# An adaLN attention and GEGLU block on one core: gate and up projections in seven products over two row groups, gates folded into the weights, and an order that knows which DVE and POOL instructions exclude each other

## The chip, the core and the metric

The kernel runs on one core of one Trainium2 chip. The metric is device time in microseconds (us), the median of three runs; there is one launch and no work on the host. The engines are PE (matrix products into PSUM), DVE and ACT (vector and scalar work, both read PSUM and SBUF), POOL (vector work on SBUF alone) and SP, which issues every DMA of this kernel.

## What is computed

```python
mod = (silu(c) @ w_mod).reshape(1, 6, 1, 512)          # sa, ca, ga, sb, cb, gb
h = layernorm(x) * (1 + ca) + sa                       # x: 2048 rows of 512
q = h @ wq                                             # 32 heads of 128
k, v = the last 512 rows of each head's cache
o = softmax(q @ k.T * 128 ** -0.5) @ v                 # every row sees all 512 keys
x = x + ga * (o @ wo)
h = layernorm(x) * (1 + cb) + sb
x = x + gb * ((gelu(h @ w_gate) * (h @ w_up)) @ w_down)   # 512 -> 1376 -> 512
```

## The kernel before

**Products in pairs.** Every large operand is held as two fp16 tiles, a high part and the rounding remainder (low part). A product is three fp16 matmuls into one PSUM bank: high x high, high x low, low x high. Nearly every matmul streams 512 columns. Making a pair is one ACT instruction (the high part) and one DVE or POOL instruction (value minus high part).

**Stages.** The 2048 rows are 4 row groups of 512. Attention goes over 16 pairs of heads, and for each over 2 heads x 4 row groups, 128 iterations in all, which overlap: scores (psS, two banks a tile, two tiles), maximum on DVE, exponentials on ACT, high part on ACT, low part on POOL, DMA transposes of the probabilities (pT), their product with v (psO), its pair (oT), and the product with Wo (psW), which DVE scales and adds to the 16 resident accumulators acc. From the fourth pair of heads on, the q projection of two heads and two row groups already uses seven half-size products in place of eight (PRODUCTS, with sums T1 to T4 of the activations and S1 to S4 of the weights).

Then comes the feed-forward part. For each row group acc is multiplied by ga and x is loaded again and added (x1_mul, x1_load, x1_add); the second layernorm gives a transposed pair (ln2_chunk, ln2_high, ln2_low); and for each of 11 blocks of 128 hidden columns (the last has 96) a *unit* follows: 24 gate and up matmuls into one psS tile, GELU on ACT, the product with up on DVE, the pair of the result (ff_act), and one unit later 12 matmuls with w_down into four banks that collect all 11 blocks (down). After the last block DVE multiplies by gb, POOL adds acc and the row group is stored. 4 row groups x 11 blocks are 44 units. All weight pairs are made in the first row group's units (ff_quick) and kept.

**Order.** The code doesn't issue instructions directly. A recorder (Weaver) notes each one with its operands (note), and a list scheduler (issue) then runs a small model of the engines with a cost for each instruction (cost) and emits on every engine what is ready and due first; each engine then takes its instructions strictly in that order. The recorder's line is that of every instruction in the profile (L245), so groups there are told apart by tile names. In those names numbers are left out: T and B are the named activation tiles, raw is a loaded weight block, wd a w_down pair, gl the GELU's output, hid or B its pair, y the output rows, and wm, mx, st small helpers.

## Time and profile before

| | us |
|---|---|
| median of 3 runs | 1748.34 (1746.94 to 1749.17) |
| the profiled execution, its own time | 1748.06 |
| its span, first to last instruction | 1746.3 |
| PE busy in the span | 1698.6 (97%) |
| DVE, ACT, POOL busy | 1213.4, 1081.5, 1069.3 (69, 62, 61%) |

The profile is one execution. A view by windows gives, for a stretch of the span, the busy time of each engine and the number of its instructions; a view by groups collects instructions of one kind and shape with their mean time; the timeline lists them in order, with the idle time before one and what ended it in square brackets. Attention fills the span from about 60 to about 1390 us, the feed-forward part the rest. A matmul's shown time includes its drain, during which the next one already runs, so rates are read from distances between starts.

### The profile page before, as it was taken

To read this page: it belongs to the slowest core of one execution; us is meant where nothing else is said; L and a number is where in the kernel's file an instruction comes from. 1 tells how busy PE (TensorE), PEld (TensorE's weight loads), DVE (VectorE), ACT (ScalarE), POOL (GpSimd) and SP (SyncE) were. 2 spreads that over 40 slices of the span, in tenths; PEclk is the share of its full clock that TensorE was granted. 3 is DMA by queue.
4 is the path that set the end of the run, shared out by engine and by line. 5 is a ranking of instruction groups with operands and counts; after the bars stand their busy time and mean duration, and the time that the engine had idled before them with its cause. 6 is when DMAs were issued, how large, how long until landed. Compare 5 with 4: busy or idle time off the path is not lost.

```text
span 1746.3 us, 23696 instructions
## 1 busy us (share of the span) xinstructions
PE 1698.6 (97%) x7927; PEld 785.7 (45%) x7927; DVE 1213.4 (69%) x2292; ACT 1081.5 (62%) x2145; POOL 1069.3 (61%) x845
## 2 busy tenths in 40 slices
...
GB/s 187 118 132 142 171 147 131 149 188 191 188 185 139 141 125 146 117 146 123 139 140 137 140 129 142 138 135 133 139 127 151 174 99 0 25 1 24 1 25 25
DMA packets 658955, 213.56 MB, mean 122 GB/s; under 512 B 580304, under 2 KB 640720, under 8 KB 658832
## 3 DMA queue, kind: packets, MB, share of 16 engines
...
q8 instruction: 63, 1.03, 0.2%
...
## 4 chain that ended last, share of the span: by engine, by line
PE 84%; DVE 6%; POOL 3%; DMA 3%; ACT 2%; issue 1%; SPq 0%; DVEq 0%; POOLq 0%; ACTq 0%
PE psS L245 30%; PE psW L245 19%; PE psO L245 19%; PE psQ L245 16%; DMA pT<-pp 3%; DVE st L245 2%; DVE acc L245 2%; POOL pp L245 1%; ACT p L245 1%; SPq L245 0%; ACT pp L245 0%; DVE mx L245 0%; DVE B L245 0%; POOL tf L245 0%; POOL A L245 0%
## 5 line engine op out<-in xcount | busy, mean ns | idle before, releaser
L245 POOL TENSOR_TENSOR pp<-p,pp 128x1024 f16<-128x1024 f32 x256 | 545.9, 2133 | 266.7 <-ACT pp L245 200.4
L245 ACT ACTIVATE p<-psS,st,es 128x512 f32<-128x512 f32 x512 | 393.1, 773 | 231.1 <-DVE st L245 224.6
L245 DVE SCALAR_TENSOR_TENSOR acc<-psW,st,acc 128x512 f32<-128x512 f32 x496 | 367.7, 743 | 120.5 <-PE psW L245 119.4
L245 PE MATMUL psW<-wo,oT 128*128 128x512 f16 x1536 | 416.4, 379 | 8.8 <-DVE oT L245 4.0
L245 PE MATMUL psS<-kT,q 128*128 128x512 f16 x1536 | 389.6, 381 | 1.1 <-DMA kT<-k 1.1
L245 PE MATMUL psO<-pT,v 128*128 128x512 f16 x1536 | 370.4, 379 | 8.1 <-DMA pT<-pp 7.7
L245 DVE TENSOR_REDUCE st<-psS 128x2 f32<-128x1024 f32 x256 | 312.7, 1222 | 79.9 <-PE psS L245 78.7
L245 ACT ACTIVATE pp<-p 128x1024 f16<-128x1024 f32 x256 | 270.7, 1058 | 3.6 <-DMA pT<-pp 0.9
L245 PEld LDWEIGHTS <-oT 128*128 128x128 f16 x1536 | 149.9, 98 | 190.9 <-issue 7.1
L245 PEld LDWEIGHTS <-v 128*128 128x128 f16 x1536 | 149.0, 98 | 192.8 <-issue 10.3
L245 PEld LDWEIGHTS <-q 128*128 128x128 f16 x1536 | 148.3, 98 | 173.3 <-issue 3.2
L245 ACT ACTIVATE gl<-psS,ffs 128x512 f32<-128x512 f32 (+1 forms) x44 | 30.2, 687 | 228.0 <-PE psS L245 228.0
L245 DVE SCALAR_TENSOR_TENSOR gl<-psS,ffs,gl 128x512 f32<-128x512 f32 (+1 forms) x44 | 32.9, 748 | 179.2 <-ACT gl L245 179.2
L245 ACT ACTIVATE oT<-psO 128x512 f16<-128x512 f32 x128 | 76.1, 594 | 90.1 <-PE psO L245 89.9
L245 PE MATMUL psQ<-B,A 128*128 128x512 f16 x528 | 130.2, 380 | 1.5 <-DVE q L245 1.5
L245 PEld LDWEIGHTS <-A 128*128 128x128 f16 x756 | 74.4, 99 | 97.1 <-issue 8.1
L245 PE MATMUL psQ<-T,S 128*128 128x512 f16 x468 | 114.6, 379 | 0.0
L245 PEld LDWEIGHTS <-B 128*128 128x128 f16 (+1 forms) x744 | 72.9, 98 | 86.0 <-issue 0.3
L245 DVE SCALAR_TENSOR_TENSOR oT<-psO,oT 128x512 f16<-128x512 f32 x128 | 87.8, 686 | 22.8 <-ACT oT L245 22.6
L245 PEld LDWEIGHTS <-T 128*128 128x128 f16 (+1 forms) x672 | 68.2, 101 | 77.2 <-issue 0.3
L245 ACT ACTIVATION_READ_ACCUMULATOR p<-psS,st,es 128x1 f32 x512 | 101.1, 197 | 0.0
L245 POOL TENSOR_TENSOR q<-h,q 128x512 f16<-128x512 f32 x78 | 90.2, 1157 | 13.8 <-ACT q L245 13.2
(194 smaller groups left out, 2062.2 us busy)
## 6 DMA issues: line engine op xcount, KB each, us to landing
...
pT<-pp SPq DMA_TRANSPOSE x512, 3.3
...
```

What stands on the lines that cost most here:

```text
L245: real(*a, **k)
```

## The change

**Seven products.** The gate and up projections of one block of hidden columns and *two* row groups become one *split unit*: with gate and up as the two rows and the two halves of the 512 inputs as the two columns of a 2 x 2 block matrix, and two row groups as the columns of the other factor, seven products of 6 matmuls each (42) stand for 48. Blocks 0 and 1 of the first two row groups stay as they were (PLAIN), so there are 4 plain units and 20 split units. The products come in four stages, (0, 6), (1), (2, 4), (3, 5), and collect in the two banks X and Y of a psS tile. After each of the first three stages ACT copies X to SBUF (h32) and DVE adds Y to such a copy (r, in stages one, three and four); GELU, product and pair follow. The activations need sums of half blocks (f_full, f_sum: ft and hf) and pairs of them (T1 to T4). The weights need four sums (aw_sum on POOL: S1f to S4f) and six pairs (aw_high on ACT, aw_low on POOL) for each of 16 split units; the 4 others use the pairs of the unit just ahead of them.

**w_down products.** Two blocks of hidden columns are collected in a bank (6 matmuls), and DVE adds the bank at once to acc, scaled by one number (down_add). acc is stored directly.

**Gates.** gb is multiplied into w_down on POOL (wd_gate) and, for the maxima that set the scale, once more during attention (fm_gate). ga is multiplied into Wo on POOL for the last 4 pairs of heads (h_gate), and into what acc has collected by then (acc_gate). x is loaded and added to acc during attention (x_load, x_add). The passes over acc between attention and the layernorm, y, and the passes over the output rows are gone.

**Order.** The scheduler's model takes new costs for SP (470 ns a load, 1290 ns a transpose, in place of 62) and for fp32 matmuls, a later landing of DMAs, a dependency between two engines that read one PSUM tile, and a lock: POOL instructions and DVE instructions with two SBUF operands (or tensor_scalar) don't overlap in it, and DVE takes another instruction first where it can.

In the program the 512-column matmuls go from 7574 to 7454, the 128-column transposes stay at 201.

```diff
-            return (110.0 if n > 8 else 60.0) * (1 if what == "transpose" or n <= 8 else n / 128) if wide else max(n, 60) / 2.4 + 2.4
+            if a[1].dtype != F32:
+                return max(n, 60) / 2.4 + 2.4
+            return 110.0 if what == "transpose" else 224.0 * max(1.0, n / 128)
...
+            alone = held[:1] == [None]
+            if alone:
                 lo, hi = -1, 1 << 30
             for e in held:
-                if e and (write or e[3]) and e[0] < hi and lo < e[1]:
+                if e and (write or e[3] or alone and self.ops[e[2]][0] != engine) and e[0] < hi and lo < e[1]:
...
+        d = (470.0 if what == "dma_start" else 1290.0) if engine == "SP" else self.cost(engine, what, a, k, n, [x.name for x in read])
+        if engine == "SP":
+            short = what == "dma_start" and any(len(x.ap) > 2 and list(x.ap)[-1][1] <= P for x in a[:2])
+            n = 1450.0 if what != "dma_start" else n * 4 * P / (195.0 if short else 390.0)
+        flat = [x for x in read if self.extent(x)[0] > 1]
+        lock = engine == "POOL" or (engine == "DVE" and not any(x.name.startswith("ps") for x in flat) and n > 2 and
+                                    (what == "tensor_scalar" or (len(flat) == 2 and what != "tensor_reduce")))
+        self.ops.append((engine, d, deps, real, a, k, n, lock))
...
-                lag = c if e == self.ops[n][0] == "PE" else c + self.LAG + (self.DRAIN if e == "PE" else 2600.0 if e == "SP" else 0.0)
+                lag = c if e == self.ops[n][0] == "PE" else c + self.LAG + (self.DRAIN if e == "PE" else 3300.0 if e == "SP" else 0.0)
...
-            n = heapq.heappop(can[e])[1]
+            aside = []
+            if e == "DVE" and shared > t + 100.0:
+                while can[e] and self.ops[can[e][0][1]][7]:
+                    aside.append(heapq.heappop(can[e]))
+                if not can[e] and wait[e] and wait[e][0][0] < shared:
+                    free[e] = wait[e][0][0]
+            pick = None if aside and free[e] > t else heapq.heappop(can[e]) if can[e] else aside.pop(0)
+            for x in aside:
+                heapq.heappush(can[e], x)
+            if pick is None:
+                continue
+            n = pick[1]
             order.append(n)
-            _, d, _, _, a, k, size = self.ops[n]
+            d, size, lock = self.ops[n][1], self.ops[n][6], self.ops[n][7]
+            if lock:
+                t = max(t, shared)
+                shared = t + d - self.NEXT[e]
             free[e] = t + d - self.NEXT[e]
...
-                whole = self.ops[n][3].__name__ == "dma_start"
-                bus = max(bus, t + 1350.0) + (size * 4 * 128 / 190.0 if whole else 1300.0)
-                end = max(bus, t + 2000.0) + 300.0
+                bus = max(bus, t + (1800.0 if d < 1000.0 else 1300.0)) + size
+                end = bus + 650.0
...
+    def h_gate(h):
+        nc.gpsimd.tensor_tensor(RAW["wo", h], RAW["wo", h], ga, op=OP.mult)
...
+                if kind == "wo" and g >= GATED:
+                    at(b + st[1], h_gate, h)
...
+    def fm_gate(n):
+        _, _, r, _ = pieces_[n]
+        m = r.stop - r.start
+        nc.gpsimd.tensor_tensor(FM[n][:m], FM[n][:m], gb[:m], op=OP.mult)
...
     for n in range(len(pieces_)):
-        at(s + 2 + 4 * n, fm_load, n)
-        at(s + 8 + 4 * n, fm_max, n)
-    s += 8 + 4 * len(pieces_)
+        at(s + 2 + 3 * n, fm_load, n)
+        if n >= 24:
+            at(s + 5 + 3 * n, fm_gate, n)
+        at(s + 8 + 3 * n, fm_max, n)
+    s += 8 + 3 * len(pieces_)
+
+
+    def acc_gate(t, eng):
+        eng.tensor_tensor(acc[t], acc[t], ga, op=OP.mult)
+
+    def x_load(t):
+        XR[t] = raw_tile("raw2", 2)
+        nc.sync.dma_start(XR[t], x[t * P:(t + 1) * P, :])
+
+    def x_add(t, eng):
+        eng.tensor_tensor(acc[t], acc[t], XR.pop(t), op=OP.add)
+
+    XR = {}
+    for t in range(SQ // P):
+        qg, j = divmod(t, 4)
+        at(2 * (PER * (GATED - 1) + 2 * qg + 5 + j) + 0.5, acc_gate, t, (nc.vector, nc.gpsimd)[j % 2])
+        at(s + 2 + 2 * t, x_load, t)
+        at(s + 8 + 2 * t, x_add, t, (nc.gpsimd, nc.vector)[t % 2])
...
+    def f_full(p, c, nm, eng):
+        t = FT[c, nm] = right.tile([P, N], F32, name="ft", tag="sa", bufs=1)
+        b = ff_b(p, nm)
+        eng.tensor_tensor(t, b[:, 0, c, :], b[:, 1, c, :], op=OP.add)
+
+    def f_sum(p, c, n, eng):
+        b12, b22 = FULL[2 * p + 1, c], FULL[2 * p + 1, c + 2]
+        z1, z2 = FT[c, "B11"], FT.get((c, "B21"))
+        o, a, b = ((z1, b12, z1), (b12, b22, b12), (b22, b22, z1), (z2, z2, b22))[n]
+        eng.tensor_tensor(o, a, b, op=OP.subtract)
...
+    def wd_gate(f, eng=nc.gpsimd):
+        m = rows(f)
+        t = FRAW["d", f]
+        eng.tensor_tensor(t[:m], t[:m], gb[:m], op=OP.mult)
...
+    def aw_sum(u, n):
+        v, h = aw_halves(u)
+        for nm in ("S1", "S2", "S3", "S4")[:n + 1]:
+            v[nm] = AW[u, nm] if (u, nm) in AW else None
+        o, a, b, op = (("S1", "A21", "A22", OP.add), ("S2", "S1", "A11", OP.subtract),
+                       ("S3", "A11", "A21", OP.subtract), ("S4", "A12", "S2", OP.subtract))[n]
+        t = AW[u, o] = right.tile([P, N // 2], F32, name=o + "f", tag=o, bufs=1)[:, :h]
+        nc.gpsimd.tensor_tensor(t, v[a], v[b], op=op)
+
...
+    def aw_low(u, nm):
+        src, t = aw_part(u, nm)
+        nc.gpsimd.tensor_tensor(t[:, 1, :], src, t[:, 0, :], op=OP.subtract)
...
+    def aw_scale(u):
+        for nm, i in (("g", 0), ("u", 1)):
+            v = FRAW[nm, u][:, :NC * rows(u[1])]
+            nc.scalar.activation(v, v, AF.Copy, scale=ffs[:, i:i + 1])
...
+    def product(u, k):
+        p, f = u
+        m = rows(f)
+        a, nm = PRODUCTS[k]
+        if k == 0:
+            PX[u] = pair()
+        pq, b, w = PX[u][:m, int(k > 3), :], ff_b(p, nm), AW[u if u in AW else (0, f)]
+        first, last = k in (0, 4, 6), k in (3, 5, 6)
+        for c in range(2):
+            o = (2 * ORDER[a] + c) * m
+            hi, lo = w[:, 0, o:o + m], w[:, 1, o:o + m]
+            for n, (x_, y_) in enumerate(((hi, b[:, 0, c, :]), (hi, b[:, 1, c, :]), (lo, b[:, 0, c, :]))):
+                nc.tensor.matmul(pq, x_, y_, start=first and (c, n) == (0, 0), stop=(c, n) == (1, 2),
+                                 skip_group_check=True)
+
...
+    def finish(u, r):
+        p, f = u
+        m = rows(f)
+        t = RT.pop((u, r))
+        nc.vector.scalar_tensor_tensor(t[:m, 1, :], t[:m, 1, :], ffs[:m, 4:5], t[:m, 0, :], op0=OP.mult, op1=OP.mult)
+        hid_high(2 * p + r, f, t[:, 1, :])
+        hid_low(2 * p + r, f, t[:, 1, :])
...
+    STAGES = ((0, 6), (1,), (2, 4), (3, 5))
+
+    def stage(u, n):
+        m = rows(u[1])
+        for k in STAGES[n]:
+            product(u, k)
+        X, Y = (PX[u][:m, i, :] for i in range(2))
+        if n < 3:
+            v = UV[u, n] = right.tile([P, N], F32, name="h32", tag="h32", bufs=3)
+            nc.scalar.activation(v[:m], X, AF.Copy)
+        if n in (0, 2):
+            t = r_tile(u, n // 2)[:m, n // 2, :]
+            nc.vector.tensor_tensor(t, Y, UV.pop((u, n))[:m], op=OP.add)
+            if n == 0:
+                gelu(u, 0, t)
+        if n == 3:
+            nc.vector.tensor_tensor(RT[u, 0][:m, 1, :], Y, UV.pop((u, 1))[:m], op=OP.add)
+            gelu(u, 1, X)
+            finish(u, 1)
+            finish(u, 0)
...
+    def down_add(pd, p, t, last):
+        a = acc[8 * p + t]
+        nc.vector.scalar_tensor_tensor(a, pd, ffs[:, 5:6], a, op0=OP.mult, op1=OP.add)
+        if last:
+            nc.sync.dma_start(out[(8 * p + t) * P:(8 * p + t + 1) * P, :], a)
...
+    UNITS = [(0, f) for f in range(PLAIN, 6)] + [(p, f) for f in range(6, NF - 1) for p in range(2)] + \
+        [(0, NF - 1)] + [(1, f) for f in range(6)] + [(1, NF - 1)]
+    SPLIT = [u for u in UNITS if not (u[0] and 6 <= u[1] < NF - 1)]
...
-        u = done[0] // (2 * NC)
-        for _ in range(2):
-            if nd < (u - 1 if u < NU else u):
-                down(nd)
-                nd += 1
-        if u < NU:
-            qg, f = divmod(u, NF)
-            if qg == 0:
...
-            fill(2 * NC)
...
+    def sums_a(p, c):
+        f_full(p, c, "B11", nc.vector)
+        f_sum(p, c, 0, nc.gpsimd)
+        f_high(p, c, "T1")
+        f_sum(p, c, 1, nc.vector)
+        f_sum(p, c, 2, nc.gpsimd)
+        f_low(p, c, "T1")
+        for nm in ("T2", "T3"):
+            f_high(p, c, nm)
+            f_low(p, c, nm)
+
+    def sums_b(p, c):
+        f_full(p, c, "B21", nc.vector)
+        f_sum(p, c, 3, nc.gpsimd)
+        f_high(p, c, "T4")
+        f_low(p, c, "T4")
...
+    for n, u in enumerate(UNITS):
+        p, f = u
+        k = SPLIT.index(u) if u in SPLIT else None
+        if k is not None:
+            if k + 4 < len(SPLIT):
+                aw_load(SPLIT[k + 4])
+            if k + 2 < len(SPLIT):
+                aw_make(SPLIT[k + 2])
+        if WDS:
+            w = WDS.pop(0)
+            wd_load(w)
+            wd_gate(w)
+            wd_high(w)
+            wd_low(w)
+        if p == 0:
+            for g, *a in P1.get(f, []):
+                g(*a)
...
+    down(len(DQ))
+    pds = {}
+    for t in (4, 5, 6, 7):
+        pds[t] = bank(("psO", "psW", "psW", "psQ")[t - 4], (1, 2, 2, 1)[t - 4])
+        down_mm(pds[t], 1, (4, 5), t, True, False)
+    for t in (4, 5, 6, 7):
+        down_mm(pds[t], 1, (NF - 1,), t, False, True)
+        down_add(pds[t], 1, t, True)
```

Three places show how instructions move; L245 before and L268 after are the recorder's line. First PE, near the end of the feed-forward part, where a unit's gate and up matmuls end. Before, the last of 24 (with weights T4_1 here) is followed by w_down matmuls of the unit ahead, and the next unit's gate and up follow these:

```order
L245 MATMUL psS_3114<-h2_3012,T4_1_3021 96x512
L245 LDWEIGHTS T4_1_3021
L245 MATMUL psS_3114<-h2_3012,T4_1_3021 96x512
L245 LDWEIGHTS B21_1_2956
L245 MATMUL psQ_3102<-wd_3022,B21_1_2956 128x512
```

In the change, the end of the w_down matmuls between stage (0, 6) and stage (1) of one split unit (psS_3381 is its tile, T2 the operand of product 1):

```order
L268 LDWEIGHTS hid_3326
L268 MATMUL psW_3384<-wd_2938,hid_3326 128x512
L268 LDWEIGHTS hid_3307
L268 MATMUL psO_3386<-wd_2929,hid_3307 128x512
L268 LDWEIGHTS hid_3307
L268 MATMUL psO_3386<-wd_2929,hid_3307 128x512
L268 LDWEIGHTS aw_3351
L268 MATMUL psS_3381<-T2_0_3103,aw_3351 128x512
```

Eight w_down matmuls (6 into psW_3384, 2 into psO_3386) stand between the last matmul of product 6 and the first of product 1, which adds to the bank that ACT has to copy first. Before, no matmul of a unit adds to a bank that another engine has just read.

Second DVE, at the passage from attention to the feed-forward part. Before, evictions of psW and psO (acc, oT) alternate with low parts of weights (raw, ffs) and passes over acc:

```order
L245 SCALAR_TENSOR_TENSOR acc_80<-psW,st,acc_80 128x512
L245 SCALAR_TENSOR_TENSOR acc_81<-psW,st,acc_81 128x512
L245 RECIPROCAL st<-st 128x4 x2
L245 SCALAR_TENSOR_TENSOR wd<-raw,ffs,wd 128x512
L245 SCALAR_TENSOR_TENSOR T_0_2972<-raw,ffs,T_0_2972 128x512 x2
L245 TENSOR_TENSOR acc_74<-acc_74,ga 128x512
L245 TENSOR_TENSOR acc_75<-acc_75,ga 128x512
L245 TENSOR_TENSOR acc_76<-acc_76,ga 128x512
L245 SCALAR_TENSOR_TENSOR oT<-psO,oT 128x512
```

In the change, a little later in the program, when the last attention rows are evicted:

```order
L268 TENSOR_TENSOR hf<-hf 128x512
L268 TENSOR_TENSOR T_1_3002<-ft,T_1_3002 128x512
L268 TENSOR_TENSOR B_1_2985<-hf,B_1_2985 128x512
L268 TENSOR_TENSOR ft<-B_1_2942 128x512
L268 TENSOR_TENSOR T_1_3004<-hf,T_1_3004 128x512
L268 TENSOR_TENSOR T_1_3003<-hf,T_1_3003 128x512
L268 TENSOR_TENSOR hf<-hf 128x512
L268 TENSOR_TENSOR T_1_3002<-ft,T_1_3002 128x512
L268 SCALAR_TENSOR_TENSOR r<-psS,ffs,r 128x512
```

The weights' low parts and the gate passes have left DVE here; sums and low parts of the activations (ft, hf, T1 to T4) have taken their place, eight in a row with two SBUF operands each.

Third POOL, in the feed-forward part. Before, in the second row group, it has little to do:

```order
L245 TENSOR_TENSOR h_3012<-h_3020,h_3012 128x512
L245 TENSOR_TENSOR h_3012<-h_3029,h_3012 128x512
L245 TENSOR_TENSOR y<-y,acc_70 128x512
L245 TENSOR_TENSOR y<-y,acc_71 128x512
L245 TENSOR_TENSOR y<-y,acc_72 128x512
```

In the change it makes the sums and low parts of one split unit's weights after another:

```order
L268 TENSOR_TENSOR S1f<-raw 128x256
L268 TENSOR_TENSOR aw<-S3f,aw 128x256
L268 TENSOR_TENSOR S2f<-S1f,raw 128x256
L268 TENSOR_TENSOR aw<-S4f,aw 128x256
L268 TENSOR_TENSOR S3f<-raw 128x256
L268 TENSOR_TENSOR S4f<-raw,S2f 128x256
L268 TENSOR_TENSOR raw<-raw,gb 128x512
L268 TENSOR_TENSOR hf<-hf,ft 128x512
L268 TENSOR_TENSOR aw<-raw,aw 128x512
L268 TENSOR_TENSOR aw<-raw,aw 128x256
```

A split unit's weights take ten such instructions (four sums, six low parts); the rows belong to two units, and the gate of a w_down block and an activation sum stand between them.

413 lines of the change are left out of this document (238 added, 175 removed).

## The prediction, written before the changed kernel was run

> **What bounds the kernel now.** I read the page first, then windows along the span, then the timeline at its two ends of interest.
>
> ```profile
> span 1746.3 us, 23696 instructions
> PE 1698.6 (97%) x7927; PEld 785.7 (45%) x7927; DVE 1213.4 (69%) x2292; ACT 1081.5 (62%) x2145; POOL 1069.3 (61%) x845
> ```
>
> Busy shares mix stages, so by windows. The columns are the stretch, its length, then the busy us with the count of instructions of PE, of PE's weight loads, of DVE, ACT and POOL, and last the granted clock, the DMA share and GB/s:
>
> ```profile
> 0.00:50.00 50.00, 35.42 (x195) 28.43 (x195) 26.89 (x68) 15.67 (x24) 16.61 (x35) 0.73 0.51 163
> 50.00:100.00 50.00, 40.81 (x194) 19.84 (x195) 43.01 (x74) 38.55 (x74) 42.51 (x34) 0.97 0.63 132
> 200.00:250.00 50.00, 49.93 (x233) 22.24 (x231) 36.38 (x73) 38.67 (x79) 44.32 (x37) 1.00 0.83 164
> 1350.00:1400.00 50.00, 41.24 (x187) 18.63 (x186) 49.50 (x84) 31.42 (x57) 29.36 (x22) 0.97 0.76 171
> 1500.00:1550.00 50.00, 50.00 (x238) 23.20 (x236) 10.19 (x14) 10.27 (x16) 1.16 (x1) 1.00 0.00 1
> 1600.00:1650.00 50.00, 50.00 (x241) 24.37 (x240) 11.14 (x15) 13.27 (x21) 1.16 (x1) 1.00 0.00 0
> ```
>
> In attention (200 to 250) PE is full, with its helpers at 73 to 89%. In the feed-forward part (1500, 1600) PE is full and every other engine nearly idle. Outside these PE loses time twice: in the first 100 us (23.8 us not busy) and at the passage between the stages (8.8 us, with DVE at 49.5 of 50). PE's own rate in the feed-forward part:
>
> ```profile
> 1720.92 5.34 PE L245 MATMUL psS<-h,T 128*128 128x512 f16 x24
> 1726.11 0.81 PE L245 MATMUL psQ<-wd,hid 128*128 128x512 f16 x3
> ```
>
> 24 matmuls in 1726.11 - 1720.92 = 5.19 us are 0.216 us each. So there a matmul taken away is 0.216 us off the end, as long as the helpers keep up.
>
> **The matmuls.** 20 split units save 6 each: 7574 - 7454 = 120, times 0.216 is **-25.9 us**. The w_down matmuls stay 528, only grouped otherwise. The Trainium skill (TensorE: Matmul & The Clock Gate, Back-to-back issue gap) gives some 131 ns for each matmul of a sustained stream of this width; by that estimate the saving would be 15.7 us. The rows above contradict it: every full window holds 233 to 241 matmuls in 50 us.
>
> **The tail.**
>
> ```profile
> 1737.76 1.46 PE L245 MATMUL psW<-wd,B 96*128 96x512 f16 x6
> 1739.65 3.08 SPq L245 DMA_DIRECT2D out_dram<-y  x4
> 1739.99 2.01 DVE L245 TENSOR_TENSOR y<-y,acc 128x512 f32<-128x512 f32 x2
> ```
>
> The last matmul ends at 1739.2; the multiplication by gb and the addition end at 1742.0, and 4.3 us of store follow. Now one eviction (0.74, row below) stands before the store: 0.03 + 0.74 + 4.3 = 5.1 in place of 7.1, **-2.0 us**. The last unit's GELU chain is covered as now: 24 matmuls of w_down (5.2 us) stand beside it.
>
> **The hand-overs inside a split unit.** A plain unit has none on PE's path; a split unit has three. The nearest chain is the last GELU of before:
>
> ```profile
> 1733.88 0.81 PE L245 MATMUL psQ<-wd,B 128*128 128x512 f16 x3
> 1734.14 0.68 ACT L245 ACTIVATE gl<-psS,ffs 96x512 f32<-96x512 f32 x1 [5.64 <-PE psS L245]
> 1734.85 0.75 DVE L245 SCALAR_TENSOR_TENSOR gl<-psS,ffs,gl 96x512 f32<-96x512 f32 x1 [5.63 <-ACT gl L245]
> 1736.29 0.69 DVE L245 TENSOR_TENSOR B<-gl,B 96x512 f16<-96x512 f32 x1 [0.70 <-ACT B L245]
> 1737.04 1.69 PEld L245 LDWEIGHTS <-B 96*128 96x128 f16 x9 [0.25 <-DVE B L245]
> ```
>
> ACT starts 0.26 us after PE's next matmul does, DVE 0.03 after ACT's end, PE 0.06 after DVE's. With copy and add priced by this view of groups:
>
> ```profile
> L245 ACT ACTIVATE h<-psQ 128x512 f32<-128x512 f32 x78 | 46.5, 596 | 10.3 <-PE psQ L245 10.3
> L245 DVE TENSOR_TENSOR y<-psW,gb 128x512 f32<-128x512 f32 x8 | 5.4, 680 | 0.0
> L245 DVE SCALAR_TENSOR_TENSOR acc<-psW,st,acc 128x512 f32<-128x512 f32 x496 | 367.7, 743 | 120.5 <-PE psW L245 119.4
> L245 DVE TENSOR_TENSOR h<-h,h 128x512 f16<-128x512 f32 x4 | 2.8, 692 | 2.3 <-ACT h L245 2.3
> L245 POOL TENSOR_TENSOR A<-raw,A 128x512 f16<-128x512 f32 x15 | 17.4, 1159 | 0.0
> L245 POOL TENSOR_TENSOR A<-raw,A 128x256 f16<-128x256 f32 x17 | 11.4, 674 | 0.0
> L245 POOL TENSOR_TENSOR raw<-raw 128x256 f32<-128x256 f32 x13 | 9.5, 730 | 0.0
> L245 POOL TENSOR_TENSOR acc<-acc,ga 128x512 f32<-128x512 f32 x4 | 5.1, 1278 | 0.0
> ```
>
> a hand-over with both engines free is 0.26 + 0.60 + 0.03 + 0.68 + 0.06 = 1.63 us, and the eight w_down matmuls that the order puts there last 8 x 0.216 = 1.73. The cover is right, by 0.1 us. It breaks when DVE is late, and what makes DVE late stands in the passage of before:
>
> ```profile
> 1358.67 2.04 DVE L245 SCALAR_TENSOR_TENSOR B<-raw,ffs,B 128x512 f16<-128x512 f32 x1
> 1361.43 0.59 PE L245 MATMUL psW<-wo,oT 128*128 128x512 f16 x2 [1.31 <-DVE acc L245]
> 1378.00 1.04 PE L245 MATMUL psW<-wo,oT 128*128 128x512 f16 x2 [4.00 <-DVE oT L245]
> 1378.58 0.73 DVE L245 SCALAR_TENSOR_TENSOR B<-raw,ffs,B 128x512 f16<-128x512 f32 x1
> ```
>
> and, as a group of that stretch (1345 to 1385 us):
>
> ```profile
> L245 DVE SCALAR_TENSOR_TENSOR B<-raw,ffs,B 128x512 f16<-128x512 f32 x4 | 5.3, 1321 | 0.0
> ```
>
> The same DVE instruction with two SBUF operands takes 0.73 us alone and 2.04 beside a POOL instruction, 1.32 in the mean of the passage: 0.59 more. The eviction queued behind it is late, and PE waits for that. Instructions that read PSUM keep their 0.74 though POOL is 61% busy. The Trainium skill (SBUF — State Buffer, Who interferes with whom) says the same: a DVE instruction with two SBUF inputs and a POOL instruction that reads SBUF exclude each other for a whole instruction. The trace agrees. The change brings just such work where POOL was idle.
>
> From the first split unit's first add to the second half's first product the order has 330 matmuls and 28 transposes, 71.3 + 3.1 = 74.4 us. (Transposes at 0.11:
>
> ```profile
> 1382.78 0.60 PE L245 MATMUL psQ<-ident,T 128*128 128x128 f32 x4
> 1383.22 1.03 PE L245 MATMUL psO<-pT,v 128*128 128x512 f16 x4
> ```
>
> four in 0.44.) DVE has 35 PSUM reads (20 x 0.743 + 15 x 0.68 = 25.1) and 42 instructions with two SBUF operands (29.5), 54.6 us or 73%. POOL has at least 38 up to the sums that T1 needs: 15 x 0.674, 13 x 0.73, 6 x 1.278 and 3 x 1.159, 30.8 us. Both kinds that exclude each other are 60 of 74 us: it fits, with little room. Later, 788 matmuls (170 us) stand beside 52 x 0.743 + 38 x 0.68 + 55 x 0.7 = 103 us of DVE, 61%. Of the 42 + 55 = 97 DVE instructions that can collide, 42% (POOL's share, 30.8 of 74.4) would by chance: 97 x 0.42 x 0.59 = 24 us of DVE lateness. That is the upper bound; zero is the lower, since the order now avoids them in its model and DVE has 20 us and 67 us of room. I take a quarter, **+6 us**, because three of the some twelve DVE instructions of a unit stand on a hand-over.
>
> **The passage.** From the last score matmul to the first add of a split unit PE has 192 matmuls and 36 transposes, 45.4 us. DVE has 24 PSUM reads (18.3), 9 statistics (6.1), 20 with two operands (13.8) and small ones (2.3), 40.5; POOL about 37 (13 x 0.674, 8 x 0.73, 7 x 1.159, 7 x 1.278, one low part of 2.13 and small ones). Excluding each other, 13.8 + 37 = 51 us in 45; with 20 x 0.59 added, DVE 52. So PE waits 6 to 7 us here, against 8.8 today. ACT is as full: 69 instructions of some 0.63 are 43 us. I take **0** for the difference; bounds -9 (all covered) and +9 (twice the excess).
>
> ```profile
> L245 DVE BATCH_NORM_STATS2 bnst<-acc 128x6 f32<-128x512 f32 x32 | 21.8, 680 | 3.8 <-DMA acc<-in_A_x_dram 3.8
> L245 POOL TENSOR_TENSOR pp<-p,pp 128x1024 f16<-128x1024 f32 x256 | 545.9, 2133 | 266.7 <-ACT pp L245 200.4 <-issue 43.0 <-POOL raw L245 10.1
> L245 ACT ACTIVATE B<-h 128x512 f16<-128x512 f32 x16 | 9.9, 629 | 4.4 <-DVE h L245 4.1
> ```
>
> **Attention and the start.** Added there: 16 gates and 16 additions on acc, half on DVE (0.68) and half on POOL (1.28), 8 Wo gates and 11 w_down gates on POOL, 16 loads on SP. That is 11 us more of DVE and 45 of POOL over 1300 us, beside a full PE and loads that are called several iterations ahead; acc's gate has the six iterations between two visits to a row group. I cost it at nothing; if the cover failed, each would delay an eviction by at most its own 1.28. The new model of SP and of the lock reorders everything:
>
> ```profile
> PE psO L245 <- DMA pT<-pp: 7.7, 12, 1.4
> L245 DVE SCALAR_TENSOR_TENSOR v<-raw,av,v 128x512 f16<-128x512 f32 x1 | 2.7, 2676 | 0.0
> ```
>
> At best the 7.7 us of waits for pT go, and two collisions of 2 us at the start, -12; at worst a new order loses as much as it gains, +5. I take **-4 us**.
>
> **Sum.** 1746.3 - 25.9 - 2.0 + 6 + 0 - 4 = 1720.4. The profiled execution took 1748.06, 1.8 more than its span, and the median is 0.3 above that: **1722 us**.
>
> **Rivals.** *The shared port decides* (chance 0.21): all the DVE lateness that isn't covered reaches PE, 15 us in place of 6, the passage loses 5 more, and the order gains nothing: 1722 + 9 + 5 + 4 = 1740, between 1731 and 1744. For it: 51 us in 45 at the passage, 60 in 74 behind it. Against: 61% DVE in the rest. *The order gains more* (0.14): SP and lock were the cause of most small waits, -12, and the hand-overs hold: 1722 - 8 - 6 = 1708. *Slower* (0.06): every one of the 60 hand-overs stands behind one more eviction (0.74) or a collision (0.59); the gain of 28 us is gone from 28 / 60 = 0.47 us of wait in each, and with 0.59 + 0.1 the time is 1748 - 28 + 41 = 1761. Against it: the order fills these places with more matmuls where its model sees DVE busy. *Nothing left* (0.04): 20 us lost at passage and hand-overs, 8 at the start: 1748. That the change doesn't remove the matmuls can be excluded: the count is in the order.
>
> **Chances.** The forecast has 0.55, own range 1714 to 1731. 1709 to 1737 leaves out the upper half of the first rival, about half of the second, and the last two. From no change this kernel can be told by about 0.2%, 3.5 us. Faster: 0.55 + 0.21 + 0.14 = 0.90; the same 0.04; slower 0.06.
>
> **What would show it.** Right: windows of some 230 matmuls in 50 us in the feed-forward part, gaps on PE behind r or h32 that sum to under 10 us, and a passage with 5 to 12 us of PE idle. Wrong: DVE's two-operand instructions at 1.3 us in the mean there and PE waiting for r in most units; or attention's windows holding fewer matmuls than now.

## The result: 1717.3 us, 1.8% less than before

The changed kernel takes 1717.3 us (median of 4 runs, 1717.08 to 1717.64); the kernel before took 1748.62 beside it (1746.94 to 1749.17). The ratio is 0.982, interval 0.981 to 0.984. The prediction said 1722, with a range of 1709 to 1737: the time lies inside, 4.7 us below the forecast. The profiled execution took 1717.18 us, its span is 1715.4, 30.9 us shorter than before (1746.3).

The page of the changed kernel:

```profile
span 1715.4 us, 24234 instructions
PE 1675.7 (98%) x7807; PEld 770.9 (45%) x7807; DVE 1298.2 (76%) x2423; ACT 1167.5 (68%) x2346; POOL 1244.5 (73%) x1033
```

The same windows as in the prediction, with the same columns, and one more of the feed-forward part (1400 to 1450):

```profile
0.00:50.00 50.00, 42.16 (x231) 31.98 (x231) 33.09 (x82) 21.54 (x36) 17.97 (x34) 0.83 0.63 185
50.00:100.00 50.00, 43.05 (x211) 20.68 (x212) 41.56 (x80) 43.45 (x84) 47.90 (x37) 1.00 0.75 149
200.00:250.00 50.00, 49.06 (x228) 21.80 (x227) 37.40 (x76) 40.35 (x83) 47.31 (x40) 1.00 0.74 149
1350.00:1400.00 50.00, 46.28 (x226) 22.27 (x225) 39.33 (x75) 43.09 (x82) 39.50 (x46) 1.00 0.47 93
1400.00:1450.00 50.00, 48.01 (x235) 23.45 (x235) 44.09 (x58) 39.38 (x72) 38.90 (x38) 1.00 0.14 42
1500.00:1550.00 50.00, 50.00 (x234) 22.63 (x232) 31.62 (x43) 24.81 (x47) 20.03 (x23) 1.00 0.14 36
1600.00:1650.00 50.00, 50.00 (x233) 22.64 (x232) 31.75 (x41) 22.77 (x47) 29.59 (x36) 1.00 0.13 47
```

Three things are to be seen. The first 50 us hold 231 matmuls where they held 195. The passage keeps PE busy for 46.28 of 50 us (41.24 before). And from 1500 us on PE is full, as before, though DVE now has 32 us of work where it had 10, and POOL 20 to 30 where it had 1. What the windows show less well is a small loss all through attention: 228 matmuls in the window from 200 us where there were 233.

For that the trace gives a finer ruler. The matmuls with 512 columns up to the 5800th are attention's in both kernels (the mix differs a little: 1506 of them are score matmuls in the change and 1495 before), so the time at which the n-th of them starts can be compared. This table holds it for all runs of this study; three differences stand beside it, attention (200th to 5800th), rest (5800th to the last) and tail (start of the last to the span's end). Rounding leaves each number open by about 0.1. The names are those of the experiments below.

| profiled execution | 200th | 5800th | last | span | attention | rest | tail |
|---|---|---|---|---|---|---|---|
| before | 104.7 | 1337.0 | 1738.8 | 1746.3 | 1232.3 | 401.8 | 7.5 |
| changed | 92.4 | 1337.3 | 1710.2 | 1715.4 | 1244.9 | 372.9 | 5.2 |
| e1, old program, new model | 91.5 | 1332.4 | 1727.0 | 1733.5 | 1240.9 | 394.6 | 6.5 |
| e2, new program, old model | 106.2 | 1347.6 | 1754.5 | 1759.0 | 1241.4 | 406.9 | 4.5 |
| e3, no lock | 97.6 | 1343.4 | 1740.0 | 1744.5 | 1245.8 | 396.6 | 4.5 |
| e4, no PSUM dependency | 91.4 | 1336.3 | 1716.3 | 1721.4 | 1244.9 | 380.0 | 5.1 |
| e5, old SP model | 91.3 | 1320.8 | 1693.5 | 1698.0 | 1229.5 | 372.7 | 4.5 |
| e6, eight products | 95.7 | 1340.3 | 1739.6 | 1744.1 | 1244.6 | 399.3 | 4.5 |
| e7, no gates, no x | 92.2 | 1332.3 | 1705.2 | 1710.4 | 1240.1 | 372.9 | 5.2 |
| e8, lock, not stepping aside | 95.4 | 1336.1 | 1712.2 | 1716.8 | 1240.7 | 376.1 | 4.6 |
| v_land | 105.9 | 1352.3 | 1723.8 | 1729.3 | 1246.4 | 371.5 | 5.5 |
| v_cost | 96.0 | 1322.7 | 1696.3 | 1702.4 | 1226.7 | 373.6 | 6.1 |
| v_lag | 92.2 | 1320.2 | 1691.6 | 1696.1 | 1228.0 | 371.4 | 4.5 |
| v_old_sp_old_fp32 | 101.1 | 1338.2 | 1710.7 | 1715.3 | 1237.1 | 372.5 | 4.6 |

So the 30.9 us are: start -12.3, attention +12.6, rest -28.9, tail -2.2. The start's gain is given back in attention almost to the microsecond, and the whole of the gain in the end comes from the passage and the feed-forward part. The experiments ask what each of these is made of.

### The profile page after: what moved, and what is told of

Its sections match the earlier page's. It is cut to its first block, busy times and chain, and to the rows that moved or that the text cites. A ratio compares the mean times of both kernels' runs of the same rounds, so it can differ in the third digit from the quotient of the medians.

```text
span 1715.4 us, 24234 instructions
## 1 busy us (share of the span) xinstructions
PE 1675.7 (98%) x7807; PEld 770.9 (45%) x7807; DVE 1298.2 (76%) x2423; ACT 1167.5 (68%) x2346; POOL 1244.5 (73%) x1033
## 4 chain that ended last, share of the span: by engine, by line
PE 68%; DVE 13%; ACT 6%; POOL 5%; DMA 4%; issue 3%; SPq 1%; DVEq 0%; ACTq 0%; POOLq 0%
PE psS L268 23%; PE psO L268 17%; PE psW L268 16%; PE psQ L268 12%; DVE st L268 5%; DVE acc L268 4%; DMA pT<-pp 3%; ACT p L268 3%; POOL pp L268 2%; ACT pp L268 1%; SPq L268 1%; DVE oT L268 1%; POOL v L268 1%; DVE mx L268 1%; ACT h L268 1%
## 5 line engine op out<-in xcount | busy, mean ns | idle before, releaser
L268 POOL TENSOR_TENSOR pp<-p,pp 128x1024 f16<-128x1024 f32 x256 | 547.1, 2139 | 216.7 <-ACT pp L268 190.2
L268 ACT ACTIVATE p<-psS,st,es 128x512 f32<-128x512 f32 x512 | 393.1, 773 | 242.5 <-DVE st L268 241.7
L268 PE MATMUL psW<-wo,oT 128*128 128x512 f16 x1536 | 458.4, 379 | 6.3 <-DVE acc L268 4.8
L268 PE MATMUL psS<-kT,q 128*128 128x512 f16 x1536 | 449.5, 379 | 13.1 <-ACT q L268 6.3
L268 PE MATMUL psO<-pT,v 128*128 128x512 f16 x1536 | 424.3, 379 | 1.1 <-DVE st L268 0.7
L268 DVE TENSOR_REDUCE st<-psS 128x2 f32<-128x1024 f32 x256 | 312.0, 1219 | 125.3 <-PE psS L268 123.6
L268 DVE SCALAR_TENSOR_TENSOR acc<-psW,st,acc 128x512 f32<-128x512 f32 x496 | 355.6, 743 | 45.7 <-PE psW L268 44.5
L268 ACT ACTIVATE pp<-p 128x1024 f16<-128x1024 f32 x256 | 270.0, 1055 | 11.9 <-DMA pT<-pp 6.6
L268 PEld LDWEIGHTS <-q 128*128 128x128 f16 x1536 | 148.6, 98 | 191.8 <-ACT q L268 13.0
L268 PEld LDWEIGHTS <-v 128*128 128x128 f16 x1536 | 149.0, 98 | 190.3 <-issue 13.6
L268 PEld LDWEIGHTS <-oT 128*128 128x128 f16 x1536 | 149.7, 98 | 185.0 <-issue 7.0
L268 PE MATMUL psQ<-B,A 128*128 128x512 f16 x528 | 147.5, 381 | 0.5 <-POOL B L268 0.5
L268 DVE SCALAR_TENSOR_TENSOR oT<-psO,oT 128x512 f16<-128x512 f32 x128 | 87.7, 685 | 68.1 <-ACT oT L268 67.9
L268 PEld LDWEIGHTS <-aw 128*128 128x128 f16 (+1 forms) x840 | 84.3, 100 | 96.9 <-issue 1.0
L268 PE MATMUL psQ<-T,S 128*128 128x512 f16 x468 | 114.9, 379 | 2.7 <-ACT h L268 2.6
L268 PE MATMUL psS<-T,aw 128*128 128x512 f16 (+1 forms) x480 | 116.3, 379 | 0.0
L268 DVE TENSOR_REDUCE mx<-raw 128x1 f32<-128x512 f32 x128 | 84.9, 671 | 37.2 <-DMA raw<-in_A_v_cache_dram 22.8
L268 PEld LDWEIGHTS <-A 128*128 128x128 f16 x756 | 72.9, 98 | 88.0 <-issue 6.4
L268 ACT ACTIVATION_READ_ACCUMULATOR p<-psS,st,es 128x1 f32 x512 | 100.8, 197 | 0.0
L268 POOL TENSOR_SCALAR raw<-raw,av 128x512 f32<-128x512 f32 x122 | 85.1, 708 | 19.3 <-DVE av L268 16.2
L268 POOL TENSOR_TENSOR q<-h,q 128x512 f16<-128x512 f32 x78 | 90.8, 1164 | 9.0 <-ACT q L268 8.5
L268 POOL TENSOR_TENSOR aw<-raw,aw 128x512 f16<-128x512 f32 (+3 forms) x32 | 33.1, 1037 | 87.3 <-ACT aw L268 87.3
```

What stands on the lines that cost most here:

```text
L268: real(*a, **k)
```

## The experiments

All times are medians; the ratio is against the kernel before, run beside it on the same chip, with its 95% interval. The recorder's line, by which the views name every instruction, moves with the code (L245 before, L268 in the change, L247 in e2, L267 in e3).

### The order alone, and the program alone

e1 is the kernel before with the new scheduler (the class Weaver of the change), e2 the changed kernel with the old one.

```diff
# e1, on the kernel before; e2 is the same the other way round, on the changed kernel
-class Weaver: as before (SP 62 ns, lag 2600, no lock, ...)
+class Weaver: as in the change (SP 470 and 1290 ns, lag 3300, lock, ...)
```

> The program of before, scheduled by the new model (SP costs, lock, PSUM dependency, fp32 cost). In the change the start gained 12.3 us by the 200th wide matmul, and attention lost 12.6 us between it and the 5800th. Theory A (the loss comes from the gates and x passes that were put into attention): without them the start's gain stays, 1748 - 12 = about 1736 us, and the 5800th matmul starts about 12 us before 1337. Theory B (the loss comes from the new order itself): the gain is given back, 1748 +- 3 us. In both the passage keeps its load of before, so its idle time stays at 8 to 10 us.

> The new program, scheduled by the old model. Theory A (order gives the start's 12 us, the added passes cost attention 12 us): the start's gain is missing and the loss stays, 1717 + 12 = about 1729 us or more. Theory B (order gives the start's gain and takes it in attention): both go, 1717 +- 3 us as far as attention is concerned. On top: if the lock matters in the feed-forward part, the gaps on PE behind matmul 6000 grow from 3 us to the 6 to 15 us of the prediction.

e1: 1737.1 us, ratio 0.993 (0.991 to 0.995). By its time theory A holds, by its trace mostly B. It gains the start's 13.2 us, loses 8.6 of it in attention without any gate or x pass there, and then gains 7.2 in passage and feed-forward, which neither theory had expected. So the order alone, without those passes, already costs attention 8.6 us.

e2: 1758.5 us, ratio 1.005 (1.003 to 1.007): slower than before, and neither theory had that. The program with 120 matmuls fewer loses time when the old model orders it. Against the change, the start is 13.8 us later, and the rest takes 34.0 us more. PE's waits there, from 1411 us on:

```profile
PE psS L247 <- DVE r L247: 21.6, 17, 4.8
```

(the columns: total wait in us, how many times, the longest). PE waits for r, the add in a hand-over, which is what the prediction had as the mechanism of its rivals.

Attention loses time in e2 as well, 9.1 us against the kernel before, under the old order. Its largest waits of PE from 100 to 1350 us are others than in the change: 8.4 us of products with v for pT and 4.5 us of products with Wo for acc. So either half of the change alone costs attention some 9 us, and both together 12.6: the parts don't add up, and the loss can't be divided between order and program.

### The lock

```diff
-        lock = engine == "POOL" or (engine == "DVE" and ...)
+        lock = False
```

> The changed kernel, with no instruction marked for the lock; all else is as in the change. If the lock is what keeps collisions off the hand-overs and out of the passage: two-operand DVE instructions get longer in the mean, PE's gaps from 1362 us on grow by 5 us or more, 1722 to 1730 us. If it is worth nothing there: 1717 +- 2 us. If the lock is what costs attention its 12 us: faster than 1717, down to 1705.

e3: 1753.0 us (1744.4 to 1755.1), ratio 1.001 (0.999 to 1.003). The direction is that of the first theory, the size far beyond it: the lock is worth 36 us by the medians, more than the whole change gains. The profiled execution took 1746.3 us, near the lower end, so the trace can account for 29 of them: 5.2 us are in the start and 23.7 in the rest. Waits of PE from 1391 to 1485 us, of e3 and then of the change:

```profile
PE psS L267 <- DVE r L267: 10.5, 4, 4.9
```

```profile
PE psS L268 <- DVE r L268: 1.1, 3, 0.5
```

One would think that without the lock DVE's instructions collide more often. The groups of DVE from 1411 us on say otherwise. Of e3:

```profile
L267 DVE SCALAR_TENSOR_TENSOR r<-r,ffs 128x512 f32<-128x512 f32 x36 | 37.7, 1074 | 0.5
L267 DVE TENSOR_TENSOR hid<-r,hid 128x512 f16<-128x512 f32 x39 | 35.1, 916 | 14.5 <-ACT hid L267 14.4
```

and of the change:

```profile
L268 DVE TENSOR_TENSOR r<-psS,h 128x512 f32<-128x512 f32 x54 | 37.1, 688 | 46.4 <-PE psS L268 26.6 <-ACT h L268 19.5
L268 DVE SCALAR_TENSOR_TENSOR r<-r,ffs 128x512 f32<-128x512 f32 x36 | 36.1, 1017 | 1.9 <-ACT r L268 1.4
L268 DVE TENSOR_TENSOR hid<-r,hid 128x512 f16<-128x512 f32 x39 | 35.1, 915 | 11.0 <-ACT hid L268 10.9
```

With two SBUF operands these take 1017 and 915 ns with the lock, and 1074 and 916 without it. Most of the collisions happen all the same (of the larger groups only the low parts of w_down are much shorter with the lock, 854 against 1035 ns, 1.4 us in all). What differs is what stands ahead of the instruction that PE needs. The longest wait is at the first matmul of the first split unit, which needs a psS tile of the last plain unit, that is, its GELU on ACT and its product on DVE. In e3:

```profile
1418.08 0.72 ACT L267 ACTIVATE wd<-raw,ffs 128x512 f16<-128x512 f32 x1 [1.04 <-POOL raw L267]
1418.71 0.67 ACT L267 ACTIVATE r<-psS,ffs 128x512 f32<-128x512 f32 x1
1421.93 0.74 DVE L267 SCALAR_TENSOR_TENSOR r<-psS,ffs,r 128x512 f32<-128x512 f32 x1
1422.72 1.86 PE L267 MATMUL psS<-B,aw 128*128 128x512 f16 x4 [4.90 <-DVE r L267]
```

and in the change:

```profile
1408.77 0.69 ACT L268 ACTIVATE r<-psS,ffs 128x512 f32<-128x512 f32 x1 [0.38 <-PE psS L268]
1409.49 0.75 DVE L268 SCALAR_TENSOR_TENSOR r<-psS,ffs,r 128x512 f32<-128x512 f32 x1 [1.17 <-ACT r L268]
1410.30 0.38 PE L268 MATMUL psS<-B,aw 128*128 128x512 f16 x1 [0.27 <-DVE r L268]
```

In e3 the GELU stands in ACT's order behind instructions that wait for POOL, and between it and the product DVE does three others, two of them with two SBUF operands; in the change ACT and DVE have nothing else to do and take both at once. At these first units DVE and POOL make the sums and low parts of the activations. The number of matmuls that the order puts between a split unit's stage (0, 6) and its stage (1) differs too (for the first four units 35, 61, 9 and 8 with the lock, and 13, 9, 9 and 9 without), but the two longest waits of e3 are not there: the second, 3.4 us, stands ahead of stage (3, 5) of the second unit, with 12 matmuls before it in e3 and 10 in the change.

These two waits cost more than themselves. Behind each, matmuls start 0.43 us apart in place of 0.216, and the granted clock falls:

```profile
1420.00:1430.00 10.00, 7.28 (x28) 3.48 (x28) 8.56 (x13) 6.76 (x11) 8.82 (x10) 0.67 0.10 26
```

(0.66 from 1457 to 1467 us; the change has 1.00 in both stretches.) That is 24 matmuls and 4.6 us. By the same ruler as in the table, 16.5 of the 23.7 us are lost between the 5800th and the 6400th matmul, up to the fifth split unit, and the other 7 in waits for r and h of at most 1.5 us.

If the order around these places is what counts, the lock should keep its worth when it is only reckoned with. e8 keeps the lock in the model's times and takes away the rule that DVE does another instruction first.

```diff
             aside = []
-            if e == "DVE" and shared > t + 100.0:
-                while can[e] and self.ops[can[e][0][1]][7]:
-                    aside.append(heapq.heappop(can[e]))
-                if not can[e] and wait[e] and wait[e][0][0] < shared:
-                    free[e] = wait[e][0][0]
```

> The changed kernel; the model still keeps locked instructions of DVE and POOL apart in its times, but DVE does not take another instruction first. Without any lock the time was 1753 us, though the two-operand DVE instructions of the feed-forward part were hardly longer (1093 against 1017 ns). If the lock helps because the model then knows how late DVE is: 1717 to 1722 us. If it helps because DVE does other work first while POOL holds the port: most of the 36 us come back, 1740 to 1753 us.

e8: 1719.7 us, ratio 0.984 (0.982 to 0.986), as the first reading expected. The matmuls behind stage (0, 6) of the first four units are 18, 66, 12 and 15 there. So nearly all of the 36 us come from a model that reckons with how late DVE and POOL will be and orders their work by that; which of the changed places in the order brings how much was not tested. Choosing another DVE instruction is worth some 2 us, which the two intervals don't tell apart from nothing.

### The PSUM dependency

```diff
-                if e and (write or e[3] or alone and self.ops[e[2]][0] != engine) and e[0] < hi and lo < e[1]:
+                if e and (write or e[3]) and e[0] < hi and lo < e[1]:
```

> The changed kernel without the dependency between two engines that read one PSUM tile. Theory B1 (this dependency delays the releases of psS and psW in attention, where PE now waits 30 times for ACT's exponentials): the waits of PE on p go and the time falls by 3 to 8 us, 1709 to 1714. Rival: it has no part in attention's loss, 1717 +- 2 us.

e4: 1722.8 us, ratio 0.985 (0.983 to 0.986). Both theories missed. It has no part in attention (1244.9 in both), and it is worth 7 us in the rest, where PE now waits for r, 4.9 us in 8 places from 1411 us on. The group of DVE's adds there (from 1411 us on; that of the change stands above) shows why:

```profile
L268 DVE TENSOR_TENSOR r<-psS,h 128x512 f32<-128x512 f32 x54 | 37.1, 688 | 56.1 <-ACT r L268 35.6 <-ACT h L268 13.3 <-PE psS L268 6.5
```

ACT r is the GELU. It and the add read two different banks of one psS tile, and neither writes to it. Still the add waits for the GELU, 35.6 us in all, where it waits for PE and for ACT's copy in the change. One such place in e4's timeline:

```profile
1566.95 0.69 ACT L268 ACTIVATE r<-psS,ffs 128x512 f32<-128x512 f32 x1 [3.16 <-issue]
1567.67 0.69 DVE L268 TENSOR_TENSOR r<-psS,h 128x512 f32<-128x512 f32 x1 [2.45 <-ACT r L268]
```

The add starts 0.03 us after the GELU's end. Two engines that read one PSUM tile take turns in this kernel, and a model that doesn't know it lets the GELU go first. The program of e4 says so too: before the add DVE waits for the count of ACT's semaphore that this GELU raises, though the add reads nothing that the GELU writes. The Trainium skill (PSUM — Partial Sum Buffer, PSUM bank collisions raise a hardware error) tells of a compiler that orders any two engines on the same bank and quadrant of partitions, reads included; here it is the tile as a whole, two banks, that the trace shows ordered.

### The matmuls

Product 6 of every split unit is issued twice, so a unit has 48 matmuls again and all else is as in the change. The product is counted twice in the sums.

```diff
-        for c in range(2):
+        seen = False
+        for c in (0, 1) if k != 6 else (0, 1, 0, 1):
...
-                nc.tensor.matmul(pq, x_, y_, start=first and (c, n) == (0, 0), stop=(c, n) == (1, 2),
+                nc.tensor.matmul(pq, x_, y_, start=first and (c, n) == (0, 0) and not seen, stop=(c, n) == (1, 2),
...
+                seen = True
```

> The changed kernel with product 6 of every split unit issued twice (its value is counted twice, so the output differs): 48 matmuls a split unit instead of 42, 120 more in all, and nothing else added. If the feed-forward part is bound by PE alone: 1717.3 + 120 x 0.216 = 1743 us. If hand-overs and collisions still cost something there, the six extra matmuls cover a part of it and it comes out at 1735 to 1741 us.

e6: 1744.6 us, ratio 0.998 (0.997 to 0.998). The rest takes 399.3 - 372.9 = 26.4 us more, against 120 x 0.216 = 25.9. The saved matmuls are worth their full time: nothing that they uncover is on the path.

### The gates and x in attention

Left out: h_gate, acc_gate, fm_gate, x_load and x_add, that is ga, x and the gate in the maxima of w_down. The output lacks ga and x.

```diff
-                if kind == "wo" and g >= GATED:
-                    at(b + st[1], h_gate, h)
...
-        if n >= 24:
-            at(s + 5 + 3 * n, fm_gate, n)
...
-        at(2 * (PER * (GATED - 1) + 2 * qg + 5 + j) + 0.5, acc_gate, t, (nc.vector, nc.gpsimd)[j % 2])
-        at(s + 2 + 2 * t, x_load, t)
-        at(s + 8 + 2 * t, x_add, t, (nc.gpsimd, nc.vector)[t % 2])
```

> The changed kernel without the gates of Wo and acc, without the gate for the maxima of w_down, and without loading and adding x (the output leaves ga and x out). Attention lost 12.6 us in the change between the 200th and the 5800th wide matmul and 8.7 with the new order alone. If the difference is the price of these passes: 1717 - 4 = 1713 us. If they are hidden, as I costed them: 1717 +- 1 us. If they are behind most of the loss: 1706 to 1709 us.

e7: 1712.0 us, ratio 0.980 (0.978 to 0.981); attention is 4.8 us shorter. The first reading holds: in this order these passes cost 5 us, and 8 us of attention's loss have another cause. The price belongs to the order: in e5 below the same passes are in, and attention is shorter than in the kernel before.

### SP's model

```diff
-        d = (470.0 if what == "dma_start" else 1290.0) if engine == "SP" else self.cost(...)
+        d = 62.0 if engine == "SP" else self.cost(...)
...
-                lag = ... 3300.0 if e == "SP" else 0.0)
+                lag = ... 2600.0 if e == "SP" else 0.0)
...
-            n = 1450.0 if what != "dma_start" else n * 4 * P / (195.0 if short else 390.0)
+            n = n * 4 * 128 / 190.0 if what == "dma_start" else 1300.0
...
-                bus = max(bus, t + (1800.0 if d < 1000.0 else 1300.0)) + size
-                end = bus + 650.0
+                bus = max(bus, t + 1350.0) + size
+                end = max(bus, t + 2000.0) + 300.0
```

> The changed kernel with the old costs of SP (62 ns an issue), the old landing model and the old lag of DMAs; lock, PSUM dependency and fp32 cost stay. Theory S (the start's gain of 12 us comes from the SP model): the 100th wide matmul starts 12 us later than in the change, at about 78 us; if attention's give-back is only the planner catching up, the end is at 1717 +- 3 us all the same, if not at 1729. Rival (the start's gain comes from the lock or the fp32 cost): the start stays as in the change, and the time at 1717 +- 3 us.

e5: 1702.9 us, ratio 0.974 (0.973 to 0.976): 14 us faster than the change, which none of the readings had. The start keeps its gain (91.3 at the 200th matmul), so that isn't SP's; and attention takes 1229.5 us, 15.4 less than in the change and 2.8 less than before, with the gates and x in it. With lock, PSUM dependency and fp32 cost in place, the new SP model is what makes attention lose. Where PE waits most from 100 to 1350 us, first in the change, then in e5:

```profile
PE psS L268 <- ACT p L268: 5.9, 30, 0.6
PE psW L268 <- DVE acc L268: 3.8, 6, 1.7
PE psQ L268 <- ACT h L268: 2.6, 6, 0.5
```

```profile
PE psO L268 <- DMA pT<-pp: 4.3, 6, 1.5
PE psQ L268 <- ACT h L268: 0.8, 1, 0.8
```

The change has removed the waits for pT that the prediction named (7.7 us), and has new ones in their place: score matmuls wait for ACT, which has yet to read the exponentials' input out of the psS tile that they are to overwrite. A timeline of the kernel before, rows on psS only, shows the rhythm as it was:

```profile
579.49 1.46 PE L245 MATMUL psS<-kT,q 128*128 128x512 f16 x6
580.98 1.23 DVE L245 TENSOR_REDUCE st<-psS 128x2 f32<-128x1024 f32 x1 [0.54 <-PE psS L245]
582.77 0.77 ACT L245 ACTIVATE p<-psS,st,es 128x512 f32<-128x512 f32 x1
583.53 0.78 ACT L245 ACTIVATE p<-psS,st,es 128x512 f32<-128x512 f32 x1
584.67 1.46 PE L245 MATMUL psS<-kT,q 128*128 128x512 f16 x6
...
589.85 1.46 PE L245 MATMUL psS<-kT,q 128*128 128x512 f16 x6
```

Six scores every 5.18 us, into the two psS tiles in turn. The tile of 579.49 is written again at 589.85, 5.5 us after its second exponential has ended (584.31). In the change:

```profile
590.47 0.59 PE L268 MATMUL psS<-kT,q 128*128 128x512 f16 x2
590.89 1.23 DVE L268 TENSOR_REDUCE st<-psS 128x2 f32<-128x1024 f32 x1 [1.07 <-PE psS L268]
591.34 0.38 PE L268 MATMUL psS<-kT,q 128*128 128x512 f16 x1
591.99 1.03 PE L268 MATMUL psS<-kT,q 128*128 128x512 f16 x4
593.65 0.78 ACT L268 ACTIVATE p<-psS,st,es 128x512 f32<-128x512 f32 x1 [2.45 <-DVE st L268]
594.42 0.77 ACT L268 ACTIVATE p<-psS,st,es 128x512 f32<-128x512 f32 x1
595.33 0.38 PE L268 MATMUL psS<-kT,q 128*128 128x512 f16 x1 [0.16 <-ACT p L268]
```

Two tiles are filled one right after the other, and the first of them is wanted back at once; PE waits until ACT is done. The waits that the view lists are only a part, since a late matmul hides in the shown time of the one before it. Added up over attention, from each start that comes over 0.02 us later than 0.216 us after the one before, the score matmuls lose 12.2 us in the change (0.2 before, 0.4 in e5). Of these, 10.4 us are lost in 29 places where the first score of a tile starts within 0.12 us of the end of ACT's last reading of that tile; e5 has no such place. The products with Wo and for q lose 9.7 us (0.2 and under 1), and the products with v 1.1 (11.2 and 7.9). So of the 15.4 us between the change and e5 the reuse of psS is the largest part, some 10 us; of the other new waits, most is made up by the waits for pT that went.

In the mean over attention the last scores of an iteration come 17.6 us before its first product with v in the kernel before, and 25.4 us in the change: a model that thinks every DMA dearer and later calls the scores earlier, and psS has no third tile for that.

The order of the programs states it without any time. From the last score into a psS tile to the first score of that tile's next use it is so many matmuls, transposes included, without the first and last iterations of attention (the last column is a mean):

| | least (1%) | 10% | median | lead of the scores, matmuls |
|---|---|---|---|---|
| before | 31 | 37 | 43 | 81 |
| changed | 21 | 21 | 36 | 115 |
| e5, all of SP's model old | 31 | 37 | 43 | 81 |
| v_cost, only issue costs old | 31 | 34 | 43 | 89 |
| v_lag, only the lag old | 24 | 28 | 39 | 91 |
| v_land, only the landing model old | 21 | 21 | 36 | 116 |

Maximum and exponentials take 0.49 + 2.03 + 1.94 = 4.5 us at e5's mean rates (last score to maximum, maximum to first exponential, two exponentials of 0.97), and 21 matmuls are 4.5 us: no slack at all in a tenth of the cases. From that the last three rows were forecast. The sum is a little too long: in the rows above the second exponential starts 0.76 us after the first, and by e5's trace the pair takes 1.64 us and the whole chain 4.2 in the mean. The slack is thus 0.3 us and not nothing, and the chain is longer in the change itself, 5.0 us in the mean, since maximum and exponentials are late there.

### SP's model, part by part

```diff
# v_land: only n, bus and end as in e5
# v_cost: only d = 62.0 as in e5 (the test d < 1000.0 in bus then asks for dma_start by name)
# v_lag: only 2600.0 as in e5
```

> The changed kernel with only the landing model of DMAs as before (issue costs of 470 and 1290 ns and the lag of 3300 stay). Theory D (reuse distance: the SP model pulls the scores ahead, so that in a tenth of the cases only 21 matmuls, 4.5 us, lie between the last score of a psS tile and the first score of the tile's next use, which is just what maximum and exponentials take, 0.49 + 2.03 + 1.94 = 4.5 us; any delay of DVE or ACT is then a wait of PE): here the order keeps 21, so nothing is regained, 1717 +- 3 us. Rival (the landing model misjudges the transposes and so the order of SP): 1703 to 1706 us.

> The changed kernel with only SP's issue costs as before (62 ns); lag and landing model stay. Theory D: the smallest reuse distance is 31 matmuls (6.7 us) again, so attention's loss goes as with the whole old SP model: 1703 to 1706 us, with no waits of PE for p. Rival (landing model or lag): 1714 to 1720 us.

> The changed kernel with only the lag of DMAs as before (2600 ns in place of 3300). Theory D: the smallest reuse distance is 24 matmuls, 5.2 us, 0.7 more than the chain takes: most of the waits for p go, 1704 to 1710 us. Rival (the issue costs as such): 1714 to 1720 us.

v_cost: 1703.1 us, ratio 0.974 (0.973 to 0.976), as forecast. v_lag: 1697.4 us, ratio 0.970 (0.969 to 0.972), below the 1704 to 1710 that were forecast. Their attention takes 1226.7 and 1228.0 us, and no wait of PE for p is left. Those of v_lag:

```profile
PE psW L268 <- DVE acc L268: 3.6, 4, 1.6
PE psO L268 <- DMA pT<-pp: 1.1, 2, 0.6
PE psW L268 <- ACT oT L268: 0.6, 1, 0.6
```

v_land: 1731.2 us, ratio 0.990 (0.989 to 0.992), 14 us above the forecast. In attention it does what the theory says, 1246.4 us and the largest wait for p:

```profile
PE psS L268 <- ACT p L268: 9.1, 37, 1.0
```

Its 14 us are lost in the start (105.9 at the 200th matmul), about which the theory says nothing. There the old landing model together with the new costs gives an order that the old or the new model as a whole doesn't.

The parts fit one number. When the scheduler works out by when an instruction is due (rank), it reckons for a transpose the issue cost, 0.06 us and the lag together: 1.29 + 0.06 + 3.30 = 4.65 us in the change and in v_land, 3.95 in v_lag, 3.42 in v_cost, and 2.72 in e5 and before. What the change's trace shows is, from the start of the issue to the landing, 3.3 us in the median:

```profile
pT<-pp SPq DMA_TRANSPOSE x512, 3.3
```

So the new lag already holds the issue, which the new issue cost adds once more. Attention takes 1244.9 and 1246.4 us where the sum is 4.65, and 1228.0, 1226.7 and 1229.5 where it is 3.95, 3.42 and 2.72. What pulls the scores too far ahead is thus not a dearer and truer model, but two figures that are each right and overlap.

v_lag is the fastest kernel of this study: one number of the change set back, 51 us below the kernel before and 20 below the change.

### The fp32 cost and the start

```diff
# on top of e5
-            return 110.0 if what == "transpose" else 224.0 * max(1.0, n / 128)
+            return (110.0 if n > 8 else 60.0) * (1 if what == "transpose" or n <= 8 else n / 128) if wide else ...
```

> The changed kernel with the old SP model and the old cost of fp32 matmuls as well; lock and PSUM dependency stay. Theory F (with SP's model gone, what is left of the start's gain, 12.6 us at the 100th wide matmul, is from the fp32 cost, since the first 50 us hold nearly all fp32 matmuls): the 100th starts at 78 to 80 us and the time is 1703 + 10 to 12 = 1713 to 1715 us. Rival (it is from the lock, in which the loaded weights' passes on DVE and POOL take part): no change, 1703 +- 3 us.

1714.4 us (1711.3 to 1718.4), ratio 0.981 (0.979 to 0.983): as theory F forecast; its profiled execution took 1717.1 us and that of e5 1699.8. The first 50 us, beside 42.16 in the change and 35.42 before:

```profile
0.00:50.00 50.00, 36.97 (x198) 29.41 (x199) 28.33 (x71) 16.09 (x25) 17.39 (x37) 0.73 0.55 174
```

198 matmuls and a granted clock of 0.73, as before, where the change has 231 and 0.83. How much of the start's gain is the higher clock and how much fewer waits isn't separated. Of the longer span 9.8 us are there at the 200th matmul; 7.6 more are in attention, where the cause stays open. The two executions lie 17.3 us apart and the medians 11.5, so most of these 7.6 us may be the spread of the runs.

Put in order, the medians give what each part of the change is worth when they are added one after another: new program with the old model 1758.5; with lock and PSUM dependency 1714.4; with the fp32 cost 1702.9; with SP's costs, lag and landing 1717.3, or without the new lag 1697.4.

## Why the prediction was right, and where it wasn't

**The matmuls, -25.9.** Right. e6 puts 120 matmuls back and the rest grows by 26.4 us.

**The tail, -2.0.** Right: 7.5 to 5.2, -2.2 us.

**The hand-overs, +6, and the passage, 0.** Mis-sized, by 9 us together. The rest is 28.9 us shorter, 25.9 of them matmuls, so passage and hand-overs gained 3.0 where the sum had them lose 6. The 3 us are the passage: PE's idle time from 1350 to 1450 us is 5.7 us in the change and 8.8 before, where the second half of that stretch is full:

```profile
1400.00:1450.00 50.00, 50.00 (x236) 22.86 (x234) 35.10 (x65) 15.87 (x27) 3.91 (x4) 1.00 0.26 76
```

The working had the passage nearly right, 6 to 7 us of waits, and then took 0 for the difference to 8.8. The hand-overs cost nothing. Yet the size that went into the upper bound was right. It took the delay of a two-operand DVE instruction as 0.42 x 0.59 = 0.25 us; measured it is 1.017 - 0.73 = 0.29 us for the products and 0.915 - 0.69 = 0.23 for the low parts. With T (8, 1044 ns) and wd (8, 854 ns) of the rows

```profile
L268 DVE TENSOR_TENSOR T<-hf,T 128x512 f16<-128x512 f32 x8 | 8.4, 1044 | 0.0
L268 DVE SCALAR_TENSOR_TENSOR wd<-raw,ffs,wd 128x512 f16<-128x512 f32 x8 | 6.7, 854 | 0.3 <-ACT wd L268 0.3
```

the lateness of these 91 instructions is 36 x 0.29 + 39 x 0.23 + 8 x 0.35 + 8 x 0.12 = 23 us, against 24 for 97; smaller groups add a little. (Two slips in that working change nothing: the POOL terms it lists are 37 instructions and not 38, and 30.8 of 74.4 is 41%.) The step that failed is "I take a quarter": PE felt none of it. Waits of PE from 1411 us on, all of them:

```profile
PE psQ L268 <- ACT T L268: 0.3, 1, 0.3
PE psS L268 <- DVE r L268: 0.3, 1, 0.3
```

The add that a hand-over needs reads PSUM and keeps its 688 ns; before it DVE stands idle and waits for PE and ACT, 46.4 us in all, so the late work ahead of it has room. That sum alone proves nothing, for without the lock it is larger, and PE waits for r all the same, 14.6 us in 11 places (e3, from 1411 us on):

```profile
L267 DVE TENSOR_TENSOR r<-psS,h 128x512 f32<-128x512 f32 x54 | 37.0, 687 | 55.4 <-PE psS L267 30.7 <-ACT h L267 24.0
```

What counts is whether each single add has that room, and this the order decides. The estimate of 1.63 us for a hand-over held as well: eight matmuls are the least that the order has behind stages (0, 6) and (2, 4), five behind stage (1), where only ACT's copy stands between, and no wait of PE is left from 1460 us on.

**The rival of the shared port** was put down as a matter of chance (0.21). It was a matter of one line: without the lock its waits appear (14.6 us for r, against 0.3) and the time goes beyond its 1731 to 1744, to 1753. The slower rival's 1761 is near what the new program gives with the old order (1758.5), but that time is made otherwise: not by 0.69 us at each of 60 hand-overs, but by 21.6 us of waits for r in 17 places, with a start that is 13.8 us later than in the change. The prediction treated the scheduler's model as an extra that may bring 4 us; it is what makes the change a gain.

**Attention and the start, -4, between -12 and +5.** The sum was right to 4 us (+0.3) and both parts of it were wrong. The start gained 12.3 us, as much as the lower bound of the whole term; it comes largely from the fp32 cost (9.8 us on top of e5), which the prediction did not price at all. Attention lost 12.6. "I cost it at nothing" fails for the gates and x in this order: 4.8 us in attention (e7), though PE is full beside them. One of its own signs of being wrong is there too, attention's windows with fewer matmuls than before (228 against 233). And "at best the 7.7 us of waits for pT go" came true, and brought a new wait with it: the prediction asked what the new SP model removes, and not what it calls earlier and which buffer that fills. 15.4 us of attention go when it is taken back (e5).

The final time was thus nearer than its parts, and that is luck: 9 us too dear in the feed-forward part, 4 too cheap ahead of it, and ahead of it a gain and a loss of 12 us that cancel.
